# The third matrix's products in a gated MLP: sums formed in place, two chains interleaved

## The chip, the cores and the metric

One core of one Trainium2 chip runs the whole program. The metric is the device time of one execution in microseconds. TensorE (PE) multiplies, VectorE (DVE), ScalarE (ACT) and GpSimd (POOL) work on what it leaves; SyncE (SP) issues most transfers, GpSimd those that add to their destination.

## The reference

```python
X = np.fft.rfft(x, axis=1)                       # x: 2 x 3008 x 256
x = np.fft.irfft(X * (filt_r + 1j * filt_i), n=3008, axis=1)   # -> 6016 x 256
h = x @ w_in;  x = (h / (1 + exp(-h))) @ w_out   # first MLP, d_ff 2048
g = x @ w_gate                                   # second MLP, d_ff 1536
return (g / (1 + exp(-g)) * (x @ w_val)) @ w_out2
```

All in float32. The change touches the second MLP alone, above all its last product with `w_out2`.

## The kernel before, in words

A float32 product is made of three passes of a shorter format: each operand is split into a high part (ScalarE, line 1082 for the third matrix's) and a low part (VectorE, line 1087), and high times high, high times low and low times high are summed in PSUM. Products of matrices are cut in two both ways and made of seven products of half size instead of eight, with sums of operands ahead of them and sums of results behind them. The seven are numbered 1 to 7; `PARTS` names the three passes.

The second MLP, called the gated stage below, works in six blocks of tokens (five of 1024, the last of 896), each in six units `u` (`Pair`). A unit makes seven gate products and seven value products, 42 matmuls on line 827, each over half of the block's tokens. Their PSUM banks come in turn from `next_bank`. `Gate.p15` makes products 1 and 5, `p6`, `p3`, `p7` and `p4` the others; line 861 copies the first product into bank `y`, lines 888 and 894 add on VectorE, line 894 into a tile `c`. Value's product 4 of a unit (`tail`) and the multiplication behind it (`join`) stand in the next unit. What a unit leaves are two tiles, `a` (named `ga`, multiplied by value on lines 1030 and 1033) and `v.c` (lines 984 and 991), each holding two blocks of the operand of the third matrix.

Two units make a chain `c`: its seven products with `w_out2`, three passes and two halves of the contraction each, are 42 matmuls on line 1131, made while later units run. Each unit calls `tick` seven times; a tick queues three of these matmuls, and issues the splits, sums and weight loads that lie some ticks ahead of them. `product` takes matmuls from the queue between its own, one to two. A chain has 14 ticks. Before the change the operands 6 and 7 have a tile of their own, `x6`, filled by copies on SP's queue (lines 1067 and 1068, `copy7`); sums of operands are accumulating transfers on GpSimd's queue (line 1071, `more`). `after7` adds the products up, in part on GpSimd (line 1125).

The order on every engine is the order of the program. `side(k)` in a unit issues what `todo2` lists for step k: the loads of weight sums `wst` for a later unit (`load_s2`), loads and splits of the next block's input (`load_x2`, `prep_x2` on GpSimd, `split_x2`, whose low part is line 796), and `store2`, which transposes a finished half of an output block on VectorE (line 1169) and stores it with eight transfers of 128-byte pieces (line 1172). Tiles come from pools: `mp` with 33 buffers for most of the above, `late` with 9 for `ga` and the third matrix's weights `w7`. A new tile takes a buffer whose last user stands earlier in the program and waits for that user.

Of the kernel before, what the change touches and what calls it, by code (L numbers as in the profile page):

```python
# [119 lines left out]
def fft_filter_mlp_kernel(  # L120
# [61 lines left out]
    def mid(shape, name, dtype=F32):  # L182
        return mp.tile(shape, dtype, tag="mid", name=name)
# [349 lines left out]
            nc.sync.dma_start(d, w.bitcast(F32))  # L533
        ready.append([])

    AT7 = (1, 5, 6, 2, 7, 3, 4)
    MINUS = (5, 2, 4)

    def pieces(q, keys, v):
        w = mid([P, len(keys), 2, 2, P], "wst", F32R)  # L540
# [218 lines left out]
    def size2(t):  # L759
        return min(STEP2, NTOK - STEP2 * t)  # L760
# [77 lines left out]
    def bank(i):  # L838
        if i not in held:
            held[i] = psum("bk")  # L840
        return held[i]

    def next_bank(name):
        n = next(turns)
        return bank(4 + n % 4 if n < 6 else (4, 5, 6, 7, 3)[(n - 4) % 5])

    class Gate:

# [4 lines left out]
        def add(self, o, k, **kw):  # L853
            product(o, lambda part: self.w(k, part), self.x(k), **kw)
# [110 lines left out]
    class Pair:  # L965
# [15 lines left out]

        def upper(self):
            o = slice(self.g.n, 2 * self.g.n)
            nc.vector.tensor_tensor(self.v.c[:, o], self.v.c[:, o], self.g.c[:, o], op=ALU.mult)

        def tail(self):
            self.v.p4()

        def join(self):
            o = slice(0, self.g.n)  # L990
            nc.vector.scalar_tensor_tensor(
                self.v.c[:, o], self.v.y, -1.0, self.g.c[:, o], op0=ALU.mult, op1=ALU.mult
            )

        def run(self, old, side):
            g, v = self.g, self.v
            n, m = g.n, 2 * g.n

            owed[0], owed[1] = 0.0, max(0.5, (len(queue) + 24 * isinstance(old, Wide) + 1e-6) / 42)
            g.p15()  # L1000
            if old:
                old.tail()
            side(-1)
            tick()
            g.p6()
            if old:
                old.join()
            side(0)
            tick()
            g.add(g.a, 2, last=True)  # L1010
            a = late["p"].tile([P, STEP2], F32, tag="mid", name="ga")
            nc.scalar.activation(a[:, :n], g.a, AF.Silu)
            if isinstance(old, Wide):
                old.second()
            g.p3()
            nc.scalar.activation(a[:, n:m], g.b, AF.Silu)
            tick()
            g.p7()
            side(1)
            tick()  # L1020
            v.p15()
            nc.scalar.activation(g.c[:, n:], g.c[:, n:], AF.Silu)
            g.p4()
            nc.scalar.activation(g.c[:, :n], g.y, AF.Silu)
            side(2)
            tick()
            v.p6()
            side(3)
            v.add(v.a, 2, last=True)
            nc.vector.tensor_tensor(a[:, :n], v.a, a[:, :n], op=ALU.mult)  # L1030
            tick()
            v.p3()
            nc.vector.scalar_tensor_tensor(a[:, n:m], v.b, -1.0, a[:, n:m], op0=ALU.mult, op1=ALU.mult)
            v.p7()
            self.upper()
            raw[self.u] = a, v.c
            tick()
            side(4)
# [2 lines left out]
            self.tail()  # L1041
            self.join()

    raw, x6, ops7, w7, low7, done7 = {}, {}, {}, {}, {}, {}
    AHEAD = 4
    clock = [-21]
    def where(i):
        c, r = divmod(i, 14)
        return c, AT7[r // 2], r % 2

    def view(c, k, p):
        u = 2 * c + p
        n = size2(u // 6) // 2
        a, b = raw[u]
        if k in (6, 7):
            return x6[c, k][:, p, :n]
        v, l = {1: (a, 0), 5: (a, 1), 2: (b, 0), 4: (b, 0), 3: (b, 1)}[k]
        return v[:, n * l:n * l + n]

    def copy7(c, p):  # L1060

        if p == 0:
            for k in (6, 7):
                x6[c, k] = mid([P, 2, 512], "x6")
        u = 2 * c + p
        n = size2(u // 6) // 2
        nc.sync.dma_start(view(c, 7, p), raw[u][0][:, n:2 * n])
        nc.sync.dma_start(view(c, 6, p), view(c, 3, p))

    def more(c, k, j, p):  # L1070
        nc.gpsimd.dma_start(view(c, k, p), view(c, j, p), accum_op=ALU.add)  # L1071

    SUMS = {
        -9: [(copy7, 0)], -7: [(copy7, 1), (more, 5, 1, 0)], -6: [(more, 5, 1, 1)],
        -5: [(more, 7, 3, 0)], -4: [(more, 6, 5, 0)], -3: [(more, 6, 5, 1)], -2: [(more, 7, 3, 1)],
        5: [(more, 4, 6, 0)], 6: [(more, 4, 6, 1)],
    }

    def high7(c, k, p):
        x = ops7[c, k, p] = mid([P, 2, 512], "ho", F32R)  # L1080
# [3 lines left out]
    def lower7(c, k, p):  # L1084
        x, v = ops7[c, k, p], view(c, k, p)
        n = v.shape[-1]
        nc.vector.tensor_tensor(x[:, 1, :n], v, x[:, 0, :n], op=ALU.subtract)  # L1087
        if k == 4:
            del raw[2 * c + p]

    def load7(c, r):
        q = c % 3
        w = late["p"].tile([P, 2, 512], F32R, tag="mid", name="w7")
        n = min(2, 7 - 2 * r)
        nc.sync.dma_start(w[:, :n].bitcast(F32), d7[q][:, 2 * r:2 * r + n])
        for i in range(n):
            w7[c, AT7[2 * r + i]] = w[:, i].rearrange("p (j l c) -> p j l c", j=2, l=2)

    def after7(c, k):
        t, q = divmod(c, 3)  # L1100
        n = size2(t) // 2
        a, b, y = (bank(i)[:, :n] for i in range(3))
        add = lambda o, v, w: nc.vector.tensor_tensor(o, v, w, op=ALU.add)
        if k == 1:
            nc.scalar.copy(y, a)
        elif k == 5:
            done7[c] = sp.tile([P, 2, STEP2 // 2], F32, name="s")
            nc.scalar.copy(done7[c][:, 0, :n], b)
        elif k == 6:
            nc.scalar.copy(done7[c][:, 1, :n], y)  # L1110
        else:
            m, l, v = {2: (0, 0, a), 3: (0, 1, b), 7: (1, 1, y), 4: (1, 0, y)}[k]
            if (t, m) not in turned:
                turned[t, m] = mid([P, 2, 512], "oa")
            o = turned[t, m][:, l, :n]
            if k in (2, 4):
                if q == 0:
                    nc.scalar.copy(o, v)
                else:
                    add(o, v, o)  # L1120
            else:
                s = done7[c][:, int(k == 3), :n]
                add(o if q == 0 else s, v, s)
                if q:
                    nc.gpsimd.tensor_tensor(o, o, s, op=ALU.add)

    def product7(c, k, p, i):
        n = size2(c // 3) // 2
        o = bank({1: 0, 2: 0, 5: 1, 3: 1, 6: 2, 7: 2, 4: 2}[k])[:, :n]
        wpart, xpart = PARTS[i]  # L1130
        nc.tensor.matmul(  # L1131
            o, w7[c, k][:, p, wpart], ops7[c, k, p][:, xpart, :n],
            start=(k in (1, 5) and p == 0 and i == 0), stop=(k in (2, 3, 4) and p == 1 and i == 2),
            skip_group_check=True,
        )
        if p == 1 and i == 2:
            after7(c, k)

    CHAINS = 3 * NBLK2

    def tick():
        i = clock[0]
        clock[0] += 1
        inside = lambda i: 0 <= i < 14 * CHAINS
        if inside(i):
            queue.extend((product7, *where(i), k) for k in range(3))
        if inside(i + AHEAD - 1):
            lower7(*where(i + AHEAD - 1))
        if inside(i + AHEAD):
            high7(*where(i + AHEAD))  # L1150
        for o in (0, 14):
            c, r = divmod(i + o, 14)
            if 0 <= c < CHAINS and r - o in SUMS:
                for fn, *args in SUMS[r - o]:
                    fn(c, *args)
        if inside(i + 8):
            c, r = divmod(i + 8, 14)
            if r % 4 == 0:
                load7(c, r // 4)

    turned = {}

# [106 lines left out]
        at(END1 - 9 + k, prep_x2, 0, k)  # L1269
    for n, k in ((-7, 1), (-6, 2), (-5, 5), (-4, 6), (-2, 3)):  # L1270
        at(END1 + n, split_x2, 0, k, True)
    for n in range(4):
        at(END1 - 6 + n, load_s2, n // 2, KV[n % 2])

    todo2 = {}
    later = lambda u, k, fn, *args: todo2.setdefault((u, k), []).append((fn, args))
# [1 line left out]
        for n, args in enumerate((("g", q), ("v", q), ("a22", q))):  # L1278
            later(2 * q - 2, n, load_2, *args)
    for u in range(6 * NBLK2):  # L1280
        later(u, 1, load_s2, u + 2, "g")
        later(u, 4, load_s2, u + 2, "v")
    later(0, -1, split_x2, 0, 7)
    later(0, 0, split_x2, 0, 4)
    for t in range(1, NBLK2):
        for m in range(2):
            later(6 * t + 3 + m, 1, store2, t - 1, m)
        u = 6 * t - 6
        later(u + 2, 0, load_x2, t)
        later(u + 3, 1, prep_x2, t, 0)  # L1290
        later(u + 3, 3, prep_x2, t, 1)
        for k, n in ((0, 1), (1, 5), (3, 6)):
            later(u + 4, k, split_x2, t, n)

        for k, n in ((3, 2), (4, 3), (4, 7)):
            later(u + 5, k, split_x2, t, n)
        later(u + 6, 0, split_x2, t, 4)
# [33 lines left out]
    with tc.manual_schedule():  # L1331
# [191 lines left out]
            now.run(old, side)  # L1523
            old = now
        old.finish()
        while clock[0] < 14 * CHAINS:
            tick()
            drain(0)
        for m in range(2):
# [42 lines left out]
```

## Time and profile before

| what | value |
|---|---|
| median of 3 runs | 1214.3 us (1210.79 to 1216.09) |
| the profiled execution's own time | 1222.56 us |
| its span, first to last instruction | 1220.7 us |
| TensorE busy | 1139.6 us (93%) |
| VectorE, ScalarE, GpSimd busy | 832.6, 790.2, 453.1 us |
| DMA traffic | 237.93 MB, mean 195 GB/s |
| mean granted clock of TensorE | 0.971 of full |

A busy share is the time in which an engine had an instruction running, over the span. Matmuls overlap, so that TensorE's share says little about how fast they follow each other; the granted clock, the waits and the time of a unit say more. Durations below come from this one execution.

### The profile page before, as it was taken

How to read it: one execution, taken by the hardware profiler on the slowest of the kernel's cores; microseconds unless marked ns; L12 is line 12 of the kernel's file. 1: busy time of each engine (PE TensorE's matmuls, PEld its weight loads, DVE VectorE, ACT ScalarE, POOL GpSimd, SP SyncE). 2: the span in 40 equal slices, each digit the busy share in tenths (PEclk: the TensorE clock that was granted, in tenths of full speed). 3: DMA queues.
4: the chain of work that ended last, by engine and by line, in shares of the span. 5: the costliest groups of instructions: out<-in, count | busy, mean ns of one | idle time of the engine just before them, and what ended most of it. 6: DMA issues, size and time to landing. Idle time of an engine off the chain costs nothing.

```text
span 1220.7 us, 15570 instructions
## 1 busy us (share of the span) xinstructions
PE 1139.6 (93%) x4993; PEld 925.8 (76%) x4993; DVE 832.6 (68%) x1271; ACT 790.2 (65%) x1491; POOL 453.1 (37%) x423
## 2 busy tenths in 40 slices
PE   9999999999999999999989997888899699889984
PEld 7588888988888878888767776666677477668873
DVE  5977455665776867866557775776578567668755
ACT  5798666676776776765566575655676466566652
POOL 3558646543513625321041334134234223313323
PEclk9999999999999999999999998999999889899987
DMA  9964442463454554455398997898799879789886
GB/s 252 283 196 125 144 156 78 138 211 130 172 165 147 189 174 157 154 180 184 119 284 216 257 253 184 224 247 216 178 270 234 189 229 267 191 209 268 200 207 120
DMA packets 161217, 237.93 MB, mean 195 GB/s; under 512 B 60272, under 2 KB 92400, under 8 KB 161136
## 3 DMA queue, kind: packets, MB, share of 16 engines
q1 hardware_dynamic: 139952, 199.78, 51.2%
q0 software_dynamic: 20736, 36.97, 17.5%
q8 instruction: 39, 0.64, 0.2%
q14 instruction: 42, 0.34, 0.1%
q10 hardware_dynamic: 448, 0.20, 0.1%
HBM read 138.99 MB, written 42.47 MB: 149 GB/s over the span
## 4 chain that ended last, share of the span: by engine, by line
PE 67%; DMA 10%; DVE 9%; ACT 5%; issue 5%; POOL 2%; POOLq 0%; DVEq 0%; ACTq 0%
PE bk L827 15%; PE acc L740 14%; PE bk L1131 7%; PE acc L717 6%; PE h L667 6%; PE y L827 5%; DMA x<-ga 5%; PE xb L827 4%; PE xa L827 4%; DMA c<-x 3%; DMA ga<-ga 3%; PE s L209 2%; DVE ho L1087 2%; PE s L397 2%; PE s L206 1%
## 5 line engine op out<-in xcount | busy, mean ns | idle before, releaser
L827 PE MATMUL bk<-xo,wst 128*128 128x512 f32 (+1 forms) x864 | 288.4, 397 | 16.7 <-ACT bk L861 11.9
L1131 PE MATMUL bk<-ho,w 128*128 128x512 f32 (+1 forms) x756 | 286.3, 401 | 3.7 <-DVE ho L1087 2.3
L740 PE MATMUL acc<-h,w 128*128 128x512 f32 x768 | 283.6, 389 | 0.0
L827 PE MATMUL bk<-xo,w 128*128 128x512 f32 (+1 forms) x648 | 220.3, 407 | 46.0 <-DVE c L894 45.6
L827 PEld LDWEIGHTS bk<-xo,wst 128*128 128x128 f32 x864 | 166.3, 194 | 59.0 <-ACT bk L861 17.9
L827 PEld LDWEIGHTS bk<-xo,w 128*128 128x128 f32 x648 | 124.5, 196 | 84.6 <-DVE c L894 58.9
L1131 PEld LDWEIGHTS bk<-ho,w 128*128 128x128 f32 x756 | 148.6, 197 | 33.3 <-DVE ho L1087 3.3
L740 PEld LDWEIGHTS acc<-h,w 128*128 128x128 f32 x768 | 144.2, 188 | 29.6
L1071 POOL DMA_DIRECT2D ga<-ga x36 | 34.9, 969 | 227.6 <-DMA x<-ga 83.4
L717 PE MATMUL acc<-h,w 128*128 128x512 f32 (+1 forms) x384 | 95.4, 376 | 0.0
L1071 POOL DMA_DIRECT2D c<-x x36 | 31.4, 957 | 153.5 <-DVE ho L1087 152.9
L1082 ACT CAST ho<-c 128x512 fp32r<-128x512 f32 (+1 forms) x108 | 64.5, 610 | 36.7 <-DVE ho L1087 18.5
L667 PE MATMUL h<-xh,w 128*128 128x512 f32 (+1 forms) x248 | 83.6, 379 | 0.3 <-POOL w L503 0.3
L717 PEld LDWEIGHTS acc<-h,w 128*128 128x128 f32 x384 | 71.2, 188 | 11.2
L1087 DVE TENSOR_TENSOR ho<-c,ho 128x512 fp32r<-128x512 f32 (+1 forms) x108 | 74.4, 700 | 7.2 <-ACT ho L1082 7.1
L1082 ACT CAST ho<-x 128x512 fp32r<-128x512 f32 (+1 forms) x72 | 44.5, 619 | 49.2 <-DMA x<-ga 34.0
L827 PE MATMUL xb<-xo,wst 128*128 128x512 f32 x192 | 74.7, 391 | 1.0 <-DVE h L921 1.0
L827 PE MATMUL xa<-xo,w 128*128 128x512 f32 x192 | 75.3, 394 | 0.0
L827 PE MATMUL y<-xo,wst 128*128 128x512 f32 x192 | 74.7, 389 | 0.0
L675 DVE TENSOR_TENSOR h<-h,h 128x512 fp32r<-128x512 f32 (+1 forms) x64 | 41.4, 655 | 47.9 <-ACT h L674 46.5
L1087 DVE TENSOR_TENSOR ho<-x,ho 128x512 fp32r<-128x512 f32 (+1 forms) x72 | 51.9, 723 | 18.4 <-ACT ho L1082 18.3
L888 DVE TENSOR_TENSOR bk<-bk,u 128x512 f32<-128x512 f32 (+1 forms) x72 | 49.2, 684 | 21.4 <-PE bk L827 19.7
(157 smaller groups left out, 2341.7 us busy)
## 6 DMA issues: line engine op xcount, KB each, us to landing
w<-d SPq DMA_DIRECT2D x54, 512.0 KB, 6.4
wst<-ds_g SPq DMA_DIRECT2D x36, 512.0 KB, 5.4
wst<-ds_v SPq DMA_DIRECT2D x36, 512.0 KB, 6.2
wst<-ds SPq DMA_DIRECT2D x32, 512.0 KB, 4.6
x<-ga SPq DMA_DIRECT2D x30, 256.0 KB, 4.6
x<-c SPq DMA_DIRECT2D x30, 256.0 KB, 4.6
ga<-ga POOLq DMA_DIRECT2D x30, 256.0 KB, 6.4
x<-c POOLq DMA_DIRECT2D x30, 256.0 KB, 7.8
```

What stands on the lines that cost most here:

```text
L209: nc.tensor.matmul(o, csp[:k, mp_, r:r + n], x[xp_], start=(i == 0), stop=(i == 2))
L397: nc.tensor.matmul(ps[:, col:col + n], zt_of[c // 2, g][:, 3 * (c % 2) + t, :], c4[:, o:o + n], start=(t == 0), stop=(t == 2), skip_group_ ...
L667: nc.tensor.matmul(ps[:, :n], wt[key, f // 4, g][:, wpart, o:o + P], x[xpart][:, g, :n], start=(g == 0 and k == 0), stop=(g == 1 and k == 2),)
L675: nc.vector.tensor_tensor(h[:, 1, :n], u[:, :n], h[:, 0, :n], op=ALU.subtract)
L717: nc.tensor.matmul(a[:, :n], w[:, wpart, o:o + 128], h[:, xpart, :n], start=(f == 0 and k == 0), stop=(f == 15 and k == 2),)
L740: nc.tensor.matmul(a, w[:, wpart, o:o + 128], h[xpart][:, n * l:n * l + n], start=(f == 0 and k == 0), stop=(end and k == 1), skip_group_c ...
L827: nc.tensor.matmul(o, w(wpart), x[:, xpart, :o.shape[-1]], start=(first and k == 0), stop=(last and k == 2), skip_group_check=True,)
L888: nc.vector.tensor_tensor(self.b, self.b, self.u2, op=ALU.add)
L1071: nc.gpsimd.dma_start(view(c, k, p), view(c, j, p), accum_op=ALU.add)
L1082: nc.scalar.copy(x[:, 0, :v.shape[-1]], v)
L1087: nc.vector.tensor_tensor(x[:, 1, :n], v, x[:, 0, :n], op=ALU.subtract)
L1131: nc.tensor.matmul(o, w7[c, k][:, p, wpart], ops7[c, k, p][:, xpart, :n], start=(k in (1, 5) and p == 0 and i == 0), stop=(k in (2, 3, 4) ...
```

## The change

Operands 5, 6, 4 and 7 are formed in the buffers of `ga` and `v.c` themselves, by four sums for each half (1 += 7, then 1 += 3, then 7 += 3, then 4 += 6); the copies and `x6` are gone. The products run in another order, with 3, 7 and 4 one period of 14 ticks later than the others, between products of the next chain, and each operand is split its own number of ticks ahead (`EARLY`). The signs of some weights and of two products of gate and value are turned to fit. The third matrix has four PSUM banks of its own, gate and value share the other four. Results are added up by VectorE and ScalarE alone. The last chain's sums are VectorE's. Loads of `wst` are issued one unit ahead instead of two, at steps 0 and 3, and `store2` stands at other steps. After the last unit 33 ticks follow instead of 21.

```diff
-    AT7 = (1, 5, 6, 2, 7, 3, 4)
-    MINUS = (5, 2, 4)
+    AT7 = (1, 5, 2, 6, 3, 7, 4)
+    MINUS = (1, 6, 7, 3)
...
     def next_bank(name):
-        n = next(turns)
-        return bank(4 + n % 4 if n < 6 else (4, 5, 6, 7, 3)[(n - 4) % 5])
+        return bank(4 + next(turns) % 4)
...
-            nc.vector.tensor_tensor(self.v.c[:, o], self.v.c[:, o], self.g.c[:, o], op=ALU.mult)
+            nc.vector.scalar_tensor_tensor(
+                self.v.c[:, o], self.v.c[:, o], -1.0, self.g.c[:, o], op0=ALU.mult, op1=ALU.mult
+            )
...
-    AHEAD = 4
-    clock = [-21]
+    ORDER7 = (3, 1, 7, 5, 2, 6, 4)
+    BACK7 = (3, 7, 4)
+    EARLY = {3: 4, 1: 8, 7: 6, 5: 6, 2: 4, 6: 4, 4: 10}
+    clock = [-19]
...
     def view(c, k, p):
...
-        if k in (6, 7):
-            return x6[c, k][:, p, :n]
-        v, l = {1: (a, 0), 5: (a, 1), 2: (b, 0), 4: (b, 0), 3: (b, 1)}[k]
-        return v[:, n * l:n * l + n]
-
-    def copy7(c, p):
-
-        if p == 0:
-            for k in (6, 7):
-                x6[c, k] = mid([P, 2, 512], "x6")
-        u = 2 * c + p
-        n = size2(u // 6) // 2
-        nc.sync.dma_start(view(c, 7, p), raw[u][0][:, n:2 * n])
-        nc.sync.dma_start(view(c, 6, p), view(c, 3, p))
+        v, l = {1: (0, 0), 5: (0, 0), 6: (0, 0), 7: (0, 1), 2: (1, 0), 4: (1, 0), 3: (1, 1)}[k]
+        return raw[u][v][:, n * l:n * l + n]
 
     def more(c, k, j, p):
-        nc.gpsimd.dma_start(view(c, k, p), view(c, j, p), accum_op=ALU.add)
-
-    SUMS = {
-        -9: [(copy7, 0)], -7: [(copy7, 1), (more, 5, 1, 0)], -6: [(more, 5, 1, 1)],
-        -5: [(more, 7, 3, 0)], -4: [(more, 6, 5, 0)], -3: [(more, 6, 5, 1)], -2: [(more, 7, 3, 1)],
-        5: [(more, 4, 6, 0)], 6: [(more, 4, 6, 1)],
-    }
+        o, v = view(c, k, p), view(c, j, p)
+        if c < CHAINS - 1:
+            nc.gpsimd.dma_start(o, v, accum_op=ALU.add)
+        else:
+            nc.vector.tensor_tensor(o, o, v, op=ALU.add)
+
+    SUMS = ((-5, 1, 7), (1, 1, 3), (4, 7, 3), (8, 4, 6))
...
+    def bank7(c, k):
+        n = size2(c // 3) // 2
+        return bank({1: 0, 2: 0, 5: 2, 3: 2}.get(k, 1 + 2 * (c % 2)))[:, :n]
...
         if k == 1:
-            nc.scalar.copy(y, a)
-        elif k == 5:
+            nc.scalar.copy(bank7(c, 6), v)
+            return
...
+        if k == 5:
             done7[c] = sp.tile([P, 2, STEP2 // 2], F32, name="s")
-            nc.scalar.copy(done7[c][:, 0, :n], b)
-        elif k == 6:
-            nc.scalar.copy(done7[c][:, 1, :n], y)
+        if k in (5, 6):
+            s = done7[c][:, int(k == 6), :n]
+            if q == 0:
+                nc.scalar.copy(s, v)
+            else:
+                add(s, v, o)
+        elif k in (3, 7):
+            add(o, v, done7[c][:, int(k == 3), :n])
+        elif q == 0:
+            nc.scalar.copy(o, v)
         else:
...
-            if k in (2, 4):
-                if q == 0:
-                    nc.scalar.copy(o, v)
-                else:
-                    add(o, v, o)
-            else:
-                s = done7[c][:, int(k == 3), :n]
-                add(o if q == 0 else s, v, s)
-                if q:
-                    nc.gpsimd.tensor_tensor(o, o, s, op=ALU.add)
+            add(o, v, o)
...
-    for n in range(4):
-        at(END1 - 6 + n, load_s2, n // 2, KV[n % 2])
+    for n in range(2):
+        at(END1 - 6 + n, load_s2, 0, KV[n])
...
-        later(u, 1, load_s2, u + 2, "g")
-        later(u, 4, load_s2, u + 2, "v")
+        later(u, 0, load_s2, u + 1, "g")
+        later(u, 3, load_s2, u + 1, "v")
...
-            later(6 * t + 3 + m, 1, store2, t - 1, m)
+            later(6 * t + 3 + 2 * m, 2 - m, store2, t - 1, m)
...
-        while clock[0] < 14 * CHAINS:
+        while clock[0] < 14 * CHAINS + 14:
             tick()
             drain(0)
```

`tick` and `where` follow `ORDER7`, `BACK7` and `EARLY`; loads of `w7` are issued at ticks -6, 2, 8 and 18 of a chain instead of every fourth.

## Rows read from the trace of the kernel before

**Rows 1.** The page: busy us, share of the span and instructions.

```profile
PE 1139.6 (93%) x4993; PEld 925.8 (76%) x4993; DVE 832.6 (68%) x1271; ACT 790.2 (65%) x1491; POOL 453.1 (37%) x423
```

**Rows 2.** Stretches: length, busy PE, PEld, DVE, ACT, POOL (instructions), clock, DMA share, GB/s.

```profile
626.04:646.15 20.11, 16.86 (x61) 12.76 (x60) 10.42 (x15) 10.56 (x20) 9.74 (x9) 0.83 1.07 329
625.81:1188.11 562.30, 501.84 (x2082) 401.34 (x2081) 391.72 (x607) 348.26 (x663) 172.25 (x173) 0.95 0.88 227
917.40:931.80 14.40, 14.40 (x65) 11.80 (x64) 10.61 (x18) 10.32 (x19) 4.84 (x5) 1.00 1.02 275
1124.40:1137.78 13.38, 13.38 (x64) 11.83 (x63) 9.89 (x17) 9.61 (x19) 5.41 (x6) 1.00 1.03 281
739.53:781.90 42.37, 33.12 (x127) 25.80 (x126) 23.27 (x38) 23.25 (x43) 7.96 (x10) 0.88 0.82 201
1165.30:1187.02 21.72, 16.98 (x64) 13.95 (x63) 10.61 (x20) 10.80 (x24) 6.68 (x8) 0.84 0.91 206
691.90:709.80 17.90, 15.63 (x64) 11.34 (x63) 12.70 (x19) 9.89 (x19) 5.68 (x6) 1.00 0.91 217
763.07:781.91 18.84, 15.95 (x64) 12.78 (x63) 12.08 (x20) 12.31 (x23) 1.72 (x2) 0.91 0.76 191
1188.11:1220.70 32.59, 17.16 (x65) 13.11 (x64) 19.92 (x32) 8.82 (x18) 11.11 (x11) 0.75 0.62 126
```

**Rows 3.** TensorE's waits from 600 us on: us in total, times, longest.

```profile
PE bk L827 <- DVE c L894: 45.6, 28, 5.9
PE bk L827 <- ACT bk L861: 11.9, 11, 2.0
```

**Rows 4.** Timeline in the first slow pair: start, duration, instruction, [idle before <- releaser].

```profile
737.51 1.30 POOL L776 TENSOR_TENSOR xr<-x,xr 128x512 f32<-128x512 f32 x1
738.75 1.76 POOL L1071 DMA_DIRECT2D c<-x  x2
...
745.64 0.69 DVE L894 TENSOR_TENSOR c<-bk,s 128x512 f32<-128x512 f32 x1 [4.95 <-DMA c<-x]
...
768.16 1.65 PE L827 MATMUL bk<-xo,w 128*128 128x512 f32 x3 [2.89 <-DVE c L894]
```

**Rows 5.** Waits of ScalarE and VectorE for sums, from 600 us on.

```profile
ACT ho L1082 <- DMA x<-ga: 34.0, 20, 3.9
...
ACT ho L1082 <- DMA ga<-ga: 21.9, 9, 6.2
DVE c L894 <- DMA c<-x: 21.6, 4, 6.2
```

**Rows 6.** Timeline around two sets of eight stores, SP and POOL.

```profile
733.96 4.14 SPq L1172 DMA_DIRECT2D out_dram<-ob  x8
...
756.00 10.47 SPq L1172 DMA_DIRECT2D out_dram<-ob  x8
...
757.50 1.21 POOL L1071 DMA_DIRECT2D x<-c  x1
```

**Rows 7.** The page's transfers: issues, KB each, median us from issue to landing.

```profile
wst<-ds_g SPq DMA_DIRECT2D x36, 512.0 KB, 5.4
wst<-ds_v SPq DMA_DIRECT2D x36, 512.0 KB, 6.2
...
ga<-ga POOLq DMA_DIRECT2D x30, 256.0 KB, 6.4
x<-c POOLq DMA_DIRECT2D x30, 256.0 KB, 7.8
```

**Rows 8.** Timeline of one addition on GpSimd and VectorE's instructions around it.

```profile
694.51 0.68 DVE L1087 TENSOR_TENSOR ho<-ga,ho 128x512 fp32r<-128x512 f32 x1
...
695.74 2.38 DVE L1087 TENSOR_TENSOR ho<-ga,ho 128x512 fp32r<-128x512 f32 x1
695.96 1.59 POOL L1125 TENSOR_TENSOR oa<-oa,s 128x512 f32<-128x512 f32 x1
```

**Rows 9.** Timeline of the tail: the last transposes.

```profile
1209.55 2.22 DVE L1169 STREAM_TRANSPOSE ob<-oa 128x448 f32<-128x448 f32 x4
```

More of the change, by code (lines that the diff above doesn't have):

```diff
@@ L990, in join @@
             o = slice(0, self.g.n)
-            nc.vector.scalar_tensor_tensor(
-                self.v.c[:, o], self.v.y, -1.0, self.g.c[:, o], op0=ALU.mult, op1=ALU.mult
-            )
+            nc.vector.tensor_tensor(self.v.c[:, o], self.v.y, self.g.c[:, o], op=ALU.mult)
         def run(self, old, side):
@@ L1029, in run @@
             v.add(v.a, 2, last=True)
-            nc.vector.tensor_tensor(a[:, :n], v.a, a[:, :n], op=ALU.mult)
+            nc.vector.scalar_tensor_tensor(a[:, :n], v.a, -1.0, a[:, :n], op0=ALU.mult, op1=ALU.mult)
             tick()
             v.p3()
-            nc.vector.scalar_tensor_tensor(a[:, n:m], v.b, -1.0, a[:, n:m], op0=ALU.mult, op1=ALU.mult)
+            nc.vector.tensor_tensor(a[:, n:m], v.b, a[:, n:m], op=ALU.mult)
             v.p7()
@@ L1042, in finish, with where @@
             self.join()
-    raw, x6, ops7, w7, low7, done7 = {}, {}, {}, {}, {}, {}
-    AHEAD = 4
-    clock = [-21]
-    def where(i):
-        c, r = divmod(i, 14)
-        return c, AT7[r // 2], r % 2
+    raw, ops7, w7, done7 = {}, {}, {}, {}
+    CHAINS = 3 * NBLK2
+    ORDER7 = (3, 1, 7, 5, 2, 6, 4)
+    BACK7 = (3, 7, 4)
+    EARLY = {3: 4, 1: 8, 7: 6, 5: 6, 2: 4, 6: 4, 4: 10}
+    clock = [-19]
+    def where(i, k=None):
+        c, r = divmod(i, 14)
+        if k is None:
+            k = ORDER7[r // 2]
+        elif ORDER7[r // 2] != k:
+            return None
+        c -= k in BACK7
+        return (c, k, r % 2) if 0 <= c < CHAINS else None
     def view(c, k, p):
@@ L1087, in lower7 @@
         nc.vector.tensor_tensor(x[:, 1, :n], v, x[:, 0, :n], op=ALU.subtract)
-        if k == 4:
+        if k == 7:
+            raw[2 * c + p] = None, raw[2 * c + p][1]
+        elif k == 4:
             del raw[2 * c + p]
     def load7(c, r):
-        q = c % 3
         w = late["p"].tile([P, 2, 512], F32R, tag="mid", name="w7")
         n = min(2, 7 - 2 * r)
-        nc.sync.dma_start(w[:, :n].bitcast(F32), d7[q][:, 2 * r:2 * r + n])
+        nc.sync.dma_start(w[:, :n].bitcast(F32), d7[c % 3][:, 2 * r:2 * r + n])
         for i in range(n):
             w7[c, AT7[2 * r + i]] = w[:, i].rearrange("p (j l c) -> p j l c", j=2, l=2)
+    def bank7(c, k):
+        n = size2(c // 3) // 2
+        return bank({1: 0, 2: 0, 5: 2, 3: 2}.get(k, 1 + 2 * (c % 2)))[:, :n]
     def after7(c, k):
@@ L1101, in after7 @@
         n = size2(t) // 2
-        a, b, y = (bank(i)[:, :n] for i in range(3))
+        v = bank7(c, k)
         add = lambda o, v, w: nc.vector.tensor_tensor(o, v, w, op=ALU.add)
         if k == 1:
-            nc.scalar.copy(y, a)
-        elif k == 5:
-            done7[c] = sp.tile([P, 2, STEP2 // 2], F32, name="s")
-            nc.scalar.copy(done7[c][:, 0, :n], b)
-        elif k == 6:
-            nc.scalar.copy(done7[c][:, 1, :n], y)
-        else:
[L1112 to L1115, printed above, removed]
-            if k in (2, 4):
-                if q == 0:
-                    nc.scalar.copy(o, v)
-                else:
-                    add(o, v, o)
-            else:
-                s = done7[c][:, int(k == 3), :n]
-                add(o if q == 0 else s, v, s)
-                if q:
-                    nc.gpsimd.tensor_tensor(o, o, s, op=ALU.add)
+            nc.scalar.copy(bank7(c, 6), v)
+            return
+        m, l = {2: (0, 0), 3: (0, 1), 6: (0, 1), 7: (1, 1), 5: (1, 1), 4: (1, 0)}[k]
+        if (t, m) not in turned and k in (2, 3, 7, 4):
+            turned[t, m] = mid([P, 2, 512], "oa")
+        o = turned[t, m][:, l, :n] if (t, m) in turned else None
+        if k == 5:
+            done7[c] = sp.tile([P, 2, STEP2 // 2], F32, name="s")
+        if k in (5, 6):
[8 more added lines that the diff above has]
+            nc.scalar.copy(o, v)
+        else:
+            add(o, v, o)
     def product7(c, k, p, i):
         n = size2(c // 3) // 2
-        o = bank({1: 0, 2: 0, 5: 1, 3: 1, 6: 2, 7: 2, 4: 2}[k])[:, :n]
+        o = bank7(c, k)
         wpart, xpart = PARTS[i]
@@ L1137, in product7 @@
             after7(c, k)
-    CHAINS = 3 * NBLK2
     def tick():
@@ L1143, in tick @@
         clock[0] += 1
[L1144 to L1159, printed above, removed]
+        at7 = where(i)
+        if at7:
+            queue.extend((product7, *at7, k) for k in range(3))
+        for k in ORDER7:
+            at7 = where(i + EARLY[k] - 1, k)
+            if at7:
+                lower7(*at7)
+        for k in ORDER7:
+            at7 = where(i + EARLY[k], k)
+            if at7:
+                high7(*at7)
+        for o, k, j in SUMS:
+            c, r = divmod(i - o, 14)
+            if r < 2 and 0 <= c < CHAINS:
+                more(c, k, j, r)
+        for r, o in enumerate((-6, 2, 8, 18)):
+            c, x = divmod(i - o, 14)
+            if x == 0 and 0 <= c < CHAINS:
+                load7(c, r)
     turned = {}
```

1 line of the change is left out of this document (removed).

## The prediction

> **What bounds the kernel now.** I read the busy shares first: TensorE is busy 93% of the span [rows 1], so work moved off other engines pays only where TensorE stands still. The table by stretches says where that is [rows 2]. The change touches only the gated stage, from about 586 us to the end, in which each of 36 units runs 42 gate and value matmuls and, from the fourth unit on, 21 matmuls of the third matrix. A clean unit takes 14.4 us at a clock of 1.00, a clean unit of the last, narrower block 13.4 us. The 33 units from 625.8 to 1188.1 us would take 27 x 14.4 + 6 x 13.4 = 469 us if all were clean; they take 562.3. So about 93 us are lost there, and the tail behind them takes 32.6 us. TensorE reads 501.8 us busy of the 562.3, but that counts pipelined matmuls of some 0.39 us each; the unit times are the better measure.
>
> Where are the 93 us? In each of four blocks, the two units around the second store of the previous block are slow together: 42.4 us where two clean ones take 28.8 (the row is the first of four alike) [rows 2]. With some 13.8 us each that is 55; unit 35 loses 8 more (21.7 against 13.4). The fourth unit loses 5.7 and one later 3.5 (20.1 and 17.9 against 14.4). The other 22 lose about 21 us together.
>
> What releases TensorE there is nearly always VectorE's line 894, the sum after product 7: 45.6 us in 28 waits, the longest 5.9; ScalarE's copy on line 861 adds 11.9 [rows 3]. VectorE is not slow by itself, it is held up in order. In the timeline, L894 wants to write a new tile `c` and stands 4.95 us until an accumulating transfer into `c` from `x` lands, and TensorE starts again after it [rows 4]. The buffer is one that `x6` has just given up, and that transfer was issued late, behind GpSimd's `prep_x2` subtractions. Elsewhere ScalarE's split waits for sums: 34.0 us for those into `x`, 21.9 us for those into `ga`, and VectorE 21.6 us for those into `c` [rows 5]. Both copies stand on SP's queue, and there eight stores of `store2` took 10.47 us with sums in flight, but 4.14 us when none had been issued [rows 6].
>
> **The change, part by part.**
>
> *Copies and `x6` go.* Two per unit, 72 in all, each with an issue on SP and a landing to wait for. The chain copy, sum, sum becomes sum, sum. The time for one sum is that of the row, 6.4 us to landing [rows 7] after 0.9 us of issue [rows 4]. The room it gets: the first sum (1 += 7) stands 5 ticks ahead of the split of operand 5, the second (1 += 3) 5 ticks ahead of that of 6, the other two 8 ticks. A unit has 7 ticks, so 5 ticks are 10.3 us. VectorE's lower half must be done first, about 1 us behind the tick: 1 + 0.9 + 6.4 = 8.3 us, inside 10.3. With the 7.8 us of the slower sums [rows 7] it is 9.7, still inside. In the old order the sum into 6 had 4 ticks (8.2 us) and the one into 4 had 3 (6.2 us). So ScalarE's 56 us of waits for sums mostly end, and the wait of L894 for `x6`'s buffer has no cause left. I take the store units' 55 + 8 us off, less 1.1 us in each of five for the block's operand splits (VectorE's L796 behind ScalarE), which stay: **-58**, bounds -40 (half of ScalarE's lateness has another cause) to -63.
>
> *GpSimd's 24 additions go, VectorE gets 24 more.* Each GpSimd addition took 1.6 us, and where one ran, VectorE's L1087, otherwise 0.68, took 2.38 us [rows 8]. That is in the unit of 17.9 us. Its 3.5 us and some 9 us more in seven units where the same meeting of the two shows are to be had; two additions in each of 12 chains cost VectorE 24 x 0.6 = 14 us, mostly in its idle third (391.7 busy of 562.3 [rows 2]), but some just ahead of L894. Net **-7**, bounds -13 to +7. ScalarE loses 24 copies of 0.58 us, off the path: nothing.
>
> *Signs* move from some operations to others of the same form count: nothing.
>
> *Weights come one unit ahead, not two, and the stores move.* Now SP matters. Value's `wst` for the next unit is issued at step 3, after 30 of 42 gate matmuls, 10.2 us into a unit, and its first user is product 5 of value in the next unit, at 14.4 + 8.2 = 22.6 us. Landing takes 6.2 us [rows 7]; without stores it has 6 us to spare. The gate's own has about the same. But `store2` now goes just ahead of it. Store 0 of a block stands at step 2 of unit 6t+3: transposes and queue start it at about 11.8 us. With 4.1 us of stores the load is issued at 15.9 and lands at 22.1: no wait. With 10.5 us it lands at 28.5: a wait of 5.9 us. Store 1 stands at step 1 of unit 6t+5, starts at 8.7 us (VectorE's lag and the first transpose put 1.6 us between step and store, as ahead of the store at 733.96 [rows 6]), and the same two prices give landings of 19.0 and 25.4 us: 0 to 2.8 us. In the new order the sums into 7 and 4 are in flight around both. I take 7 us for eight stores, between the two rows: 2.5 us of wait behind store 0, none behind store 1. Five blocks have store 0: 12.5 us, with cooling 20. A wait also cools the clock (the pair of 42.4 us has 0.88 granted, a mix of 1.2 and 2.4 GHz); its second unit, of 18.8 us, waits 2.9 us at L894 and loses 4.4 in all [rows 2, 4], so I add 1.5 each. Behind the waiting product stand all of value's products and the third matrix's, and VectorE and ScalarE run dry; behind the late load on SP stand two `w7` loads, which have 8 ticks to spare: **+21**, bounds 0 and 5 x 5.9 + 4 x 2.8 + 9 x 1.5 = +54.
>
> *Four rotating PSUM banks instead of five.* Two reuses get close: gate's bank `b` follows value's `a` of the unit before (L1030), gate's `y` follows value's `b` (L1033). L1033 stands just ahead of L894 on VectorE, and product 6, which needs ScalarE's copy into `y`, comes three matmuls after the tail that needs L894; so the copy hides behind the wait that is there already. Product 5 has 13 matmuls, 3 us, after value's product 2. I take 0.15 us a unit, **+5**, bounds 0 and +0.6 us (one VectorE operation late) x 33 = +20.
>
> *The products' order.* Each PSUM bank of the third matrix now has four slots or more between read and next use, before two. TensorE waits little on L1131 in the steady part, so: nothing.
>
> *The tail.* The chains end 33 ticks after the last unit instead of 21, with 25 of them carrying products, and chain 17's eight sums are VectorE's. Counting what VectorE still has to do there: 20 lower halves, 8 sums, 12 additions, 2 joins, 42 operations at 0.55 us (four transposes take 2.22 [rows 9]) = 23.1 us, and 1.8 us for the last two products and their addition: 24.9 us. Now it is 1188.1 to 1209.6, 21.5 us. **+3**, bounds 0 (ScalarE waited for sums there too, which ends) to +8.
>
> Sum: -58 - 7 + 21 + 5 + 3 = -36; and the fourth unit, whose first sums came late behind weight loads, gives back perhaps 4 of its 5.7: **-40**. The profiled execution took 1222.6 us around its span of 1220.7 and becomes 1182; its time lies 8.3 us above the median of the three runs, so the median goes from 1214.3 to **1174**.
>
> A rule speaks against the change here. The stores were slow with sums in flight and quick without [rows 6]. The Trainium skill, "DMA: Bandwidth & Descriptors", section "Queues, rings and completion order", says that each DMA engine takes turns between the queue rows that have work, packet by packet; the two kinds of row agree with it. By that rule the stores are slow at both new places, since sums run beside them at both, the rival of slow stores below, 1207; by the row without sums the term would be nought.
>
> **Rivals.**
> - *Forecast*, 1174 within 12: the store units heal, store 0 costs a short wait. Chance 0.40.
> - *No wait for weights at all*: eight stores stay near 4.1 us, the term of 21 goes: 1153. For it, SP no longer carries the copies; against it, sums beside the stores. 0.22.
> - *Slow stores at both places*: 10.5 us each, +54 instead of +21: 1207 if all else holds; 1200 if the loads land in the 5.4 us of the gate's [rows 7] (5 x 5.1 + 4 x 2.0 + 13.5 = 47). 0.18.
> - *The change does not cure the stall*: tiles still take buffers just given up, and VectorE or ScalarE waits on a different one (a stored `ob`, a matmul's `ho`). Half of the 58 stays: 1203. 0.10.
> - *Slower*: value's weights late in every unit. Their room is 12.4 us from step 3; a landing above that makes TensorE wait once a unit. At 14.3 us it is 1.9 us x 33 = 61 us on top of the sum without store waits (1153): slower than now from there on. Against it: the median is 6.2. For it: SP issues in order and each load must wait for a buffer. 0.10.
>
> **Numbers.** 1174. The first three and half of the fourth fill the range: from 1146 (bounds of the second) to 1206. Faster by over 0.5% (6 us, about what a measurement of this kernel tells from no change: its three runs spread over 5.3 us): below 1208, 0.84; within, 0.07; slower, 0.09.
>
> **What would show it.** No SP rows of copies; ScalarE's waits for sums below 15 us; no VectorE wait for a landing ahead of L894; pairs of store units near 32 us instead of 42; TensorE or its weight loads waiting for `wst` behind store 0. L1087 without spans above 2 us. Wrong would be: units without stores above 16 us (banks, VectorE), `wst` as the releaser in every unit, or a tail above 38 us.

## The result, and the profile after

The changed kernel takes 1168.5 us in the median of three runs (1166.25 to 1172.48), 0.963 of the time before (95% interval 0.958 to 0.969): 46 us less. The prediction was 1174, range 1146 to 1206, faster with a chance of 0.84. The profiled execution took 1168.46 us around a span of 1165.7.

On the page, busy time and share of each engine after:

```profile
PE 1118.7 (96%) x4993; PEld 914.3 (78%) x4993; DVE 839.8 (72%) x1306; ACT 777.8 (67%) x1467; POOL 410.0 (35%) x388
```

TensorE issues the same 4993 matmuls; its share rises from 93% [rows 1]. The stretches that answer to [rows 2]: all units from the fourth to the last gate matmul, a clean unit, the four store pairs, the fourth unit, the unit that had held a GpSimd addition, unit 35, the fifth block's second store unit, the tail (columns as there):

```profile
626.02:1130.91 504.89, 480.65 (x2070) 388.94 (x2069) 394.45 (x626) 337.48 (x641) 142.96 (x154) 0.99 0.85 212
873.00:887.53 14.53, 14.31 (x63) 11.52 (x62) 10.47 (x18) 10.15 (x19) 4.36 (x5) 1.00 0.93 232
732.33:765.67 33.34, 29.95 (x128) 23.27 (x126) 24.80 (x41) 23.45 (x45) 6.98 (x8) 1.00 0.84 198
824.02:857.37 33.35, 29.94 (x128) 23.26 (x126) 24.81 (x41) 23.45 (x45) 6.98 (x8) 1.00 0.85 199
916.26:949.60 33.34, 29.95 (x128) 23.27 (x126) 24.79 (x41) 23.45 (x45) 6.98 (x8) 1.00 0.84 199
1008.25:1043.87 35.62, 32.65 (x128) 25.32 (x126) 24.41 (x41) 23.58 (x45) 6.98 (x8) 0.90 0.86 197
626.02:643.61 17.59, 14.71 (x55) 11.05 (x54) 9.31 (x14) 10.08 (x19) 9.44 (x9) 0.90 0.77 188
689.33:703.61 14.28, 14.28 (x65) 11.82 (x63) 10.74 (x18) 10.30 (x19) 4.36 (x5) 1.00 0.90 220
1111.45:1129.84 18.39, 14.93 (x65) 12.81 (x63) 13.27 (x25) 11.60 (x24) 5.23 (x6) 0.91 0.82 160
1023.68:1043.87 20.19, 17.70 (x65) 13.73 (x63) 14.97 (x25) 12.70 (x24) 4.36 (x5) 0.83 0.76 169
1130.91:1165.67 34.76, 18.51 (x78) 14.94 (x76) 24.08 (x45) 8.06 (x16) 0.00 (x0) 0.79 0.37 99
```

The gain lies in the units: 562.3 us became 504.9. The four store pairs took 42.4, 42.1, 45.0 and 42.8 us before and 33.3, 33.4, 33.3 and 35.6 after, 37 us less in all; unit 35 gave 3.3, the unit of 17.9 us 3.6, the fourth 2.5, and the other 11 us are spread thin. The tail grew from 32.6 to 34.8 us.

Waits from 600 us on, of TensorE, ScalarE and VectorE (us in total, times, longest):

```profile
PE bk L827 <- DVE c L893: 10.0, 14, 1.5
PE bk L827 <- ACT bk L860: 8.0, 9, 2.4
PE bk L827 <- DVE ga L1029: 5.9, 4, 1.5
...
ACT ho L1077 <- DMA ga<-ga: 20.2, 12, 4.3
...
DVE xo L796 <- ACT xo L793: 32.1, 19, 4.5
```

L893 is what was L894, L860 was L861, L1077 was L1082. TensorE's wait for the sum after product 7 fell from 45.6 to 10.0 us and that for ScalarE's copy from 11.9 to 8.0 [rows 3], VectorE's 21.6 us of waits for landings ahead of it are gone, and ScalarE's waits for sums fell from 55.9 to 20.2 us [rows 5]. TensorE waits nowhere for `wst`. What is left of a store pair is seen in the timeline of units 9 to 11 (queue SP, VectorE and TensorE, [idle before <- releaser]):

```profile
729.78 4.81 SPq L1172 DMA_DIRECT2D out_dram<-ob  x8
734.70 0.46 SPq L646 DMA_DIRECT2D wst<-ds_v  x1
...
748.82 0.69 DVE L796 TENSOR_TENSOR xo<-xr,xo 128x512 fp32r<-128x512 f32 x1 [4.48 <-ACT xo L793]
...
750.03 0.68 DVE L1029 SCALAR_TENSOR_TENSOR ga<-bk,ga 128x512 f32<-128x512 f32 x1
...
750.76 0.50 PE L827 MATMUL bk<-xo,wst 128*128 128x512 f32 x1 [1.51 <-DVE ga L1029]
...
760.09 7.84 SPq L1172 DMA_DIRECT2D out_dram<-ob  x8
```

VectorE stands 4.5 us at the low part of a block operand (L796), which it reached before ScalarE had made the high part (L793); L1029 behind it frees a bank late, and TensorE loses 1.5 us. Of the page's transfers one row (issues, KB, median us to landing, which was 6.2 before [rows 7]):

```profile
wst<-ds_v SPq DMA_DIRECT2D x36, 512.0 KB, 4.8
```

### The profile page after: what moved, and what is told of

Its sections match the earlier page's. It is cut to its first block, busy times and chain, and to the rows that moved or that the text cites. A ratio compares the mean times of both kernels' runs of the same rounds, so it can differ in the third digit from the quotient of the medians.

```text
span 1165.7 us, 15384 instructions
## 1 busy us (share of the span) xinstructions
PE 1118.7 (96%) x4993; PEld 914.3 (78%) x4993; DVE 839.8 (72%) x1306; ACT 777.8 (67%) x1467; POOL 410.0 (35%) x388
## 4 chain that ended last, share of the span: by engine, by line
PE 79%; DVE 7%; ACT 5%; DMA 4%; issue 4%; POOL 1%; DVEq 0%; ACTq 0%; SPq 0%; POOLq 0%
PE bk L827 21%; PE acc L740 15%; PE bk L1130 10%; PE acc L717 7%; PE h L667 6%; PE y L827 6%; PE xb L827 4%; PE xa L827 4%; DMA ga<-ga 3%; PE s L209 2%; PE s L206 2%; DVE ho L1082 2%; PE s L397 2%; PE s L282 1%; ACT ho L1077 1%
## 5 line engine op out<-in xcount | busy, mean ns | idle before, releaser
L827 PE MATMUL bk<-xo,wst 128*128 128x512 f32 (+1 forms) x864 | 280.4, 390 | 15.5 <-ACT bk L860 8.0
L1130 PE MATMUL bk<-ho,w 128*128 128x512 f32 (+1 forms) x756 | 278.1, 393 | 4.5 <-DVE ho L1082 2.3
L827 PE MATMUL bk<-xo,w 128*128 128x512 f32 (+1 forms) x648 | 213.3, 396 | 10.5 <-DVE c L893 10.0
L1130 PEld LDWEIGHTS bk<-ho,w 128*128 128x128 f32 x756 | 144.4, 192 | 31.4 <-DVE ho L1082 3.6
L1068 POOL DMA_DIRECT2D ga<-c x68 | 59.4, 1064 | 181.6 <-DVE ho L1082 181.4
L1077 ACT CAST ho<-ga 128x512 fp32r<-128x512 f32 (+1 forms) x144 | 87.0, 614 | 35.0 <-DMA ga<-ga 20.2
L1068 POOL DMA_DIRECT2D ga<-ga x34 | 30.2, 892 | 198.8 <-DVE c L992 57.3
L1082 DVE TENSOR_TENSOR ho<-ga,ho 128x512 fp32r<-128x512 f32 (+1 forms) x144 | 95.7, 672 | 2.3 <-ACT ho L1077 2.3
L1082 DVE TENSOR_TENSOR ho<-c,ho 128x512 fp32r<-128x512 f32 (+1 forms) x108 | 80.7, 749 | 2.6 <-ACT ho L1077 2.6
L1077 ACT CAST ho<-c 128x512 fp32r<-128x512 f32 (+1 forms) x108 | 63.9, 611 | 13.2 <-PE bk L1130 9.0
L860 ACT COPY bk<-bk 128x512 f32<-128x512 f32 (+1 forms) x72 | 41.2, 572 | 40.9 <-DVE ga L1032 24.7
```

Of the source, the lines that this page charges most:

```text
L827: nc.tensor.matmul(o, w(wpart), x[:, xpart, :o.shape[-1]], start=(first and k == 0), stop=(last and k == 2), skip_group_check=True,)
L860: nc.scalar.copy(self.y, self.a)
L1068: nc.gpsimd.dma_start(o, v, accum_op=ALU.add)
L1077: nc.scalar.copy(x[:, 0, :v.shape[-1]], v)
L1130: nc.tensor.matmul(o, w7[c, k][:, p, wpart], ops7[c, k, p][:, xpart, :n], start=(k in (1, 5) and p == 0 and i == 0), stop=(k in (2, 3, 4) ...
```

## The experiments

Two theories stood after the result. *Copies*: the store units healed because the copies no longer stand behind the stores on SP and `x6` is gone. *Buffers*: operands, results, weights `wst` and `x6` all come from one pool of 33 buffers; with two units' weights loaded ahead the pool is used up, and a new `c` (L894) has to wait for whatever is released last. Loading one unit ahead leaves two more buffers free. The kernel before was timed again beside each group of runs (medians 1216.6 to 1217.4 us); ratios are to it, with the 95% interval.

**One part alone in the kernel before: the shorter lead.**

```diff
-    for n in range(4):
-        at(END1 - 6 + n, load_s2, n // 2, KV[n % 2])
+    for n in range(2):
+        at(END1 - 6 + n, load_s2, 0, KV[n])
...
-        later(u, 1, load_s2, u + 2, "g")
-        later(u, 4, load_s2, u + 2, "v")
+        later(u, 0, load_s2, u + 1, "g")
+        later(u, 3, load_s2, u + 1, "v")
```

> The kernel before with the weight sums loaded one unit ahead at steps 0 and 3, as in the changed kernel; nothing else. Theory of the copies (the prediction's): the slow pairs come from copies that stand behind the stores on SP and from sums that land late, so they stay above 40 us and the time between 1206 and 1220. Theory of the buffers: around the stores the pool of 33 is used up, and whatever asks for a tile waits for whoever gives one back; two weight tiles fewer alive heal most of it: pairs below 36 us, no VectorE wait for a landing at L894, the time below 1192.

1179.4 us, 0.970 (0.967 to 0.973): 37 of the 46 us, with every copy, `x6` and the stores where they were. The first store pair, and the waits from 600 us on:

```profile
738.84:772.74 33.90, 30.09 (x127) 23.26 (x126) 22.42 (x37) 22.56 (x43) 7.13 (x9) 1.00 1.04 269
```

```profile
PE bk L827 <- DVE c L894: 14.7, 23, 1.1
...
ACT ho L1082 <- DMA x<-ga: 24.4, 16, 3.8
...
ACT ho L1082 <- DMA ga<-ga: 19.1, 8, 6.7
```

The pair takes 33.9 us instead of 42.4, and no wait of VectorE for a landing is left ahead of L894, though ScalarE still waits 43.5 us for sums (55.9 before). So those waits were not what held the store units, and the copies theory falls as the main cause. The short lead also has the price that the prediction named, but not behind the first stores: TensorE waits 5.0 us for `wst` in the fourth unit and 2.5 in the last.

```profile
PE bk L827 <- DMA wst<-ds_v: 7.5, 2, 5.0
```

**The same with two buffers fewer.** If the gain came from when the loads are issued, the size of the pool would not matter.

```diff
-    mp = pool("mp", 33)
+    mp = pool("mp", 31)
```

> The kernel before with weight sums one unit ahead, and the pool cut from 33 to 31 buffers, so that just the two saved tiles are taken away again. Theory of the buffers: L894's waits for a landing come back, the two units around the second store take 40 us or more together, the time is 1205 or above. Rival, the loads' new time is what helps (they no longer meet copies and sums on the DMA engines): it stays within 6 us of the 1179 of 33 buffers.

1259.1 us, 1.037 (1.034 to 1.040), 80 us more than with 33. The first store pair, and the waits:

```profile
747.95:794.67 46.72, 34.39 (x128) 26.25 (x127) 23.09 (x38) 23.42 (x44) 9.88 (x11) 0.85 0.73 183
```

```profile
PE bk L827 <- ACT bk L861: 37.6, 14, 6.8
PE bk L827 <- DVE c L894: 36.4, 25, 3.1
...
ACT ho L1082 <- DMA c<-x: 30.7, 6, 7.5
...
DVE c L894 <- DMA c<-x: 11.1, 4, 2.9
```

The slow pair is back, and worse. With the loads issued at the same steps, two buffers are worth 80 us: buffers, not the time of the loads, carry the gain. VectorE's waits ahead of L894 are back too, but most of the stall sits at ScalarE now, four times 6.8 to 7.5 us. The first of the four (POOL and ScalarE):

```profile
749.09 1.76 POOL L1071 DMA_DIRECT2D c<-x  x2
...
756.43 0.62 ACT L1082 CAST ho<-c 128x512 fp32r<-128x512 f32 x1 [7.41 <-DMA c<-x]
```

By its place in the program this split makes the high part of operand 3, into which no sum goes. Its operand lies in the tile that the first of the two transfers writes, which landed at 753.5; the split went on only when the second had landed as well, at 756.4. What the two have in common is `x6`, which both read. So ScalarE stood for a buffer, that of `x6`, at its new tile `ho`, as VectorE does at its new `c` in the kernel before. Why 31 buffers with the short lead come out 43 us above the kernel before, which holds two more weight tiles in two more buffers, is shown no further than this: two engines stand there instead of one.

**The stores moved, alone.**

```diff
-            later(6 * t + 3 + m, 1, store2, t - 1, m)
+            later(6 * t + 3 + 2 * m, 2 - m, store2, t - 1, m)
```

> The kernel before with the stores of an output block at the changed kernel's steps (half 0 at step 2 of unit 6t+3, half 1 at step 1 of unit 6t+5); nothing else. Theory of the place: the old place beside the next block's operand sums and splits makes the slow pairs, so they shrink below 36 us and the time goes below 1192. Theories of the copies and of the buffers: the copies still stand behind the stores and no buffer is saved, so 1204 to 1220, with the loss in one or two units later at most.

1236.6 us, 1.017 (1.012 to 1.021): slower. The first pair:

```profile
736.70:781.23 44.53, 34.34 (x127) 26.22 (x126) 22.84 (x37) 23.01 (x43) 7.86 (x9) 0.89 0.75 181
```

```profile
DVE c L894 <- DMA c<-x: 20.1, 4, 5.2
```

The pair is no quicker with the stores moved (42.4 before), and the waits of VectorE for a landing ahead of L894 stay: the place of the stores does not heal it.

**The additions on VectorE, alone; four banks, alone; the additions with the shorter lead.**

```diff
-                    nc.gpsimd.tensor_tensor(o, o, s, op=ALU.add)
+                    add(o, o, s)
```

> The kernel before with the 24 additions of line 1125 on VectorE instead of GpSimd; nothing else. The prediction's term: VectorE's long L1087 (2.38 us) ends, the unit of 17.9 us falls below 15.5, and the time falls by 7 (bounds: 13 less to 7 more), to some 1207. Rival: the additions on VectorE stand ahead of L894 and cost as much as they give: 1212 to 1221.

> The kernel before with weight sums one unit ahead and line 1125's additions on VectorE: two of the change's parts, with copies, x6 and five banks left. If these two are nearly all of the change: 1168 to 1176. If sums in place give something of their own (ScalarE's waits for sums, some 44 us in the kernel with the loads alone, become 20): 1176 to 1182, and 8 us or more are left to them.

```diff
-        return bank(4 + n % 4 if n < 6 else (4, 5, 6, 7, 3)[(n - 4) % 5])
+        return bank(4 + n % 4)
```

> The kernel before with four PSUM banks in turn for gate and value instead of five; nothing else. The prediction's term: 5 us more (bounds 0 and 20), some 1219, with waits of TensorE for L1030 or of ScalarE's L861 for L1033. Rival: the fifth bank was never what anything waited for: within 3 us of before and no new releaser.

The additions alone: 1218.05 us, 1.0005 (0.998 to 1.003). With the shorter lead: 1180.4 against 1179.4 without. They are worth nothing either way that these runs can show. The unit of 17.9 us still takes 18.1 with no addition on GpSimd in it; TensorE waits 2.5 us for L894 there:

```profile
690.88:708.95 18.07, 15.37 (x65) 11.43 (x63) 11.85 (x20) 9.90 (x19) 4.39 (x5) 1.00 0.90 216
```

Four banks: 1214.2 us, 0.997 (0.995 to 0.999), a little quicker. TensorE's waits from 600 us on:

```profile
PE bk L827 <- DVE c L894: 32.3, 25, 4.9
PE bk L827 <- ACT bk L861: 11.1, 11, 1.6
PE bk L827 <- DVE ga L1030: 5.8, 4, 1.5
```

The new wait for L1030 is the one that the changed kernel shows too; a second new one, 3.7 us for L1012, it does not show. Both are outweighed by L894's, which shrinks from 45.6 to 32.3, so the path pays nothing.

**All parts but the sums in place and the new order.** The shorter lead, the additions, the moved stores and the four banks together, in the kernel before (their diffs are above).

> The kernel before with all parts of the change but the sums in place and the products' order: weight sums one unit ahead, stores at the new steps, line 1125's additions on VectorE, four banks. If the loads' new time (two buffers) is the whole of the gain: 1165 to 1173. If copies, x6 and the old order still cost what the changed kernel saves beyond it: 1176 to 1186, with ScalarE's waits for sums above 30 us.

1196.0 us, 0.981 (0.977 to 0.986): outside both expectations, 16 us above the shorter lead with the additions (1180.4) and 28 above the whole change (22 by the ratios). Against the kernel with the shorter lead and the additions, units 13, 19, 25 and 31, two behind each second store, take 73 us instead of 60, and the tail 39.9 instead of 34.9. Here are the copies that the prediction had in mind. Queue SP and POOL of this kernel around unit 12 (the view cuts off the first of the eight stores):

```profile
767.95 4.53 SPq L1172 DMA_DIRECT2D out_dram<-ob  x7
...
774.45 0.47 SPq L1067 DMA_DIRECT2D x<-ga  x1
...
776.33 0.95 SPq L1067 DMA_DIRECT2D x<-ga  x1
...
780.07 0.86 POOL L1071 DMA_DIRECT2D ga<-ga  x1 [9.33 <-DMA x<-ga]
```

and of the one with the stores at their old place:

```profile
769.19 0.47 SPq L1067 DMA_DIRECT2D x<-ga  x1
...
773.20 0.86 POOL L1071 DMA_DIRECT2D ga<-ga  x1 [3.22 <-DMA x<-ga]
```

At the new place the copies stand behind the stores; 5.3 us later goes the first copy and 6.9 us later the first sum, and ScalarE's waits for sums into `ga` grow from 15.7 to 35.0 us. So the copies behind stores do cost time where the stores have been moved. In the changed kernel, which has no copies, the same four units take 57 us; that the new place is harmless there is read from this, not tried with the stores at their old steps. The sums in place with the new order are worth 22 to 28 us on top of these parts; the whole change is 8 to 12 us quicker than the shorter lead with or without the additions, a difference hardly larger than the interval of the changed kernel's three runs.

**Every store of blocks 0 to 4 issued twice,** in the changed kernel; the second goes to a spare buffer in DRAM. It tells whether weights behind a long row of stores are late by the prediction's working.

```diff
+                if t < NBLK2 - 1:
+                    nc.sync.dma_start(spare[...], o[...])
                 nc.sync.dma_start(
```

> The changed kernel with each store of blocks 0 to 4 issued twice, once into a spare buffer in DRAM, so that SP issues 16 transfers of 128-byte pieces ahead of value's weights instead of 8. The prediction's price of a late load: stores of 9.6 to 15 us put the load some 5 us past its room behind half 0 and some 7 behind half 1, 5 x 5 + 4 x 7 and some cooling: 1168 + 50 to 65 = 1218 to 1233, with TensorE released by wst. Rival: SP's lateness is covered by the other work: below 1180.

1223.7 us, 1.006 (1.004 to 1.009), 55 above the changed kernel. The waits, and the timeline behind the first row of 16, which begins at 729.35 (lines are one or two lower down here):

```profile
PE bk L828 <- DMA wst<-ds_v: 46.2, 9, 6.8
```

```profile
738.11 1.30 SPq L1178 DMA_DIRECT2D out_dram<-ob  x1
739.52 1.33 SPq L647 DMA_DIRECT2D wst<-ds_v  x1
...
747.51 1.19 PE L828 MATMUL bk<-xo,wst 128*128 128x512 f32 x2 [6.75 <-DMA wst<-ds_v]
```

The row takes 10.1 us, near the prediction's slow price of 10.5, and TensorE then waits 6.75 us where the working said 5.9. The mechanism holds; the price of eight stores was too high.

**The last chain's sums as transfers,** in the changed kernel.

```diff
-        if c < CHAINS - 1:
+        if c < CHAINS:
```

> The changed kernel with the last chain's eight sums as transfers like all others. The prediction's tail counts VectorE's operations; if VectorE bounds the tail, eight sums fewer would save 4 us: 1164. If the chain sum, split, sum bounds it, each landing of 4.5 us or more stands in a row twice where VectorE's sum took 0.6: the tail goes from 35 to 40 us or more, 1173 to 1180.

1172.2 us, 0.962 (0.957 to 0.967). From the end of unit 35 the tail takes 37.8 us instead of 35.8, but the ratio doesn't differ from 0.963. Inconclusive; at most a small gain lies in VectorE's sums there.

**The block operand's low part one step later.** L796 stood 32 us behind ScalarE; here it is issued a step behind the high part.

```diff
-            later(u + 4, k, split_x2, t, n)
+            later(u + 4, k, split_x2, t, n, True)
...
+                due, lag[:] = lag[:], []
...
+                for fn in due:
+                    fn()
```

> The changed kernel with the low part of the next block's splits (L796) issued one step after the high part, so that VectorE does not stand behind ScalarE there. In the changed kernel VectorE idles 34.5 us in 20 such waits, and units 6t+5 and 6t take 17.5 and 15.4 us. If these waits are what is left: those units fall to 15 and 14.4, and the time to 1150 to 1160. Rival: VectorE only waits elsewhere, or the additions pile up behind: within 5 us of 1168.

1166.3 us, 0.960 (0.956 to 0.963): within the noise of the changed kernel, as the rival said. The unit behind the pair takes 14.6 us instead of 15.4, but the pair's second unit, and a new wait in it, give that back:

```profile
744.97:765.72 20.75, 17.75 (x64) 13.74 (x63) 13.51 (x23) 12.84 (x24) 4.36 (x5) 0.84 0.76 167
```

```profile
ACT ho L1077 <- DVE xo L796: 3.9, 1, 3.9
```

ScalarE now waits at a new tile `ho` for the late L796, whose result is no operand of its split: it looks like a buffer that comes free late again, though only this wait shows it.

**A best version,** twice: the low parts deferred except operand 6's, the last block's first stores seven ticks earlier and its last ones on two queues in turn; then also with operand 6 split a step earlier.

```diff
-        for k, n in ((0, 1), (1, 5), (3, 6)):
-            later(u + 4, k, split_x2, t, n)
+        for k, n in ((0, 1), (1, 5), (3, 6)):
+            later(u + 4, k, split_x2, t, n, n != 6)
...
+            if clock[0] == 14 * CHAINS + 7:
+                store2(NBLK2 - 1, 0)
...
-                nc.sync.dma_start(
+                queues[i % 2].dma_start(
```

> The changed kernel with L796 one step after its high part, except for operand 6, whose input buffer a ScalarE split waited for when it was given back late; and the last block's half 0 stored as soon as product 3 of the last chain is added, half 1's eight stores issued from two queues in turn. Units 6t fall from 15.4 to 14.6 and 6t+5 stay at 17.5: 4 us; the end saves the half of 8 us of stores: 4 to 6 us. 1157 to 1162. Rival: deferred lows hold buffers longer and ScalarE waits for them again: 1164 to 1170.

> As the run before it, with operand 6 of the next block split one step earlier (step 2 of unit 6t+4, after GpSimd's subtractions are long done). If the wait of ScalarE's split of 6 for a buffer is what holds VectorE 4.5 us there, another place finds another buffer: units 6t+5 fall from 17.5 to 15.5, 1150 to 1156. Rival: it only meets another buffer's owner: within 4 us of the run before it.

1165.2 us each, 0.957 (0.953 to 0.960): both hopes missed, both rivals met. From the end of unit 35 the tail takes 32.6 us instead of 35.8. In the second version (first the pair's second unit, then the unit two later):

```profile
744.99:760.33 15.34, 14.60 (x65) 11.75 (x64) 13.62 (x23) 11.94 (x23) 4.36 (x5) 1.00 0.84 200
774.94:795.45 20.51, 17.09 (x64) 13.60 (x63) 10.93 (x18) 10.74 (x20) 4.36 (x5) 0.83 0.90 216
```

The first heals (15.3 instead of 17.5 us) and the other, 14.3 in the changed kernel, loses 6: ScalarE waits up to 4.5 us there for a sum into `ga`. Both versions have the lowest medians, 3 us under the changed kernel, which these intervals do not tell apart.

Not run: the kernel before with two buffers more and its weights two units ahead, the direct counterpart of the run with 31; the copies and `x6` taken out with the weights still two units ahead; and the changed kernel with the stores at their old steps. Read from the program alone, the changed kernel with weights two units ahead or with 32 buffers would ask for a buffer that only later work releases.

## Why the prediction was right, and where its reasons were not

**Direction and size: right**; 1168.5 lies in the forecast's own range (1174 within 12) and between it and its rival without waits (1153). Part of the closeness is luck, as the next paragraphs say: a cause that was not the main one, terms that came to nought and cancel in part, and a starting point on the high side.

**Copies and `x6`, -58: the total holds, the places and the cause do not.** The units without the fourth gave 55 us, but the units that the term named, the four pairs and unit 35, gave 40, its smaller bound; the other 15 came from units that it left alone. The step "the wait of L894 for `x6`'s buffer has no cause left" took the late transfer for the fault, and the copies' removal for the cure. The runs show that the tile waits because no buffer is free: the shorter lead alone gives 37 us and leaves the copies, and two buffers fewer take it back with 43 more. The row that should have warned is [rows 4]. L894 there is value's in unit 9, and it starts at 745.64, when the second of the two transfers has landed (745.5). That transfer has nothing to do with what L894 computes, and the unit's last tick issues it, behind L894 in the program. The description ahead says that a new tile takes a buffer whose last user stands earlier in the program; here it does not. A tile that waits for such a user had no free buffer to take, so the question was how many tiles are alive, not why one transfer is late. Taking out `x6` frees buffers as well; whether that would have healed the store units by itself, with weights two units ahead, no run shows. The term also foresaw ScalarE's waits below 15 us; they are 20.2.

**GpSimd's additions, -7: nought** (1.0005 alone). L1087's 2.38 us [rows 8] were seen, but the unit's end hung on other waits.

**Weights, +21: nought; mis-sized.** (Its own terms, 12.5 and five times 1.5, add up to 20.) Eight stores took 4.8 us at store 0, not 7, and a load lands in 4.8 (the median), not 6.2: it is issued at 734.70 and wanted at 732.3 + 8.2 = 740.5. Store 1 started 11.9 us into its unit, not 8.7, and took 7.8 us, and the load behind it was still in time. With twice the stores the predicted wait appears. The rival of slow stores at both places needed 10.5 us at each.

**Banks, +5: nought** (0.997 alone); the wait exists, 5.9 us in all, and takes the place of part of L893's. **Tail, +3:** +2.2. **The fourth unit, -4:** 2.5, and it now has 54 matmuls instead of 60.

**The starting point.** The sum was carried down from the profiled execution, 8.3 us above its median, and the 8.3 kept. The changed kernel's profiled execution lies on its median, so the span fell by 55.0 us and the median by 45.8. By spans the steps (-40) are 15 us short: weights and banks (+26) and the additions (-7) were nought, and without them the steps give -59. So the forecast came within 6 us of the median because 9 of the 15 us went into the starting point.

The rule weighed against the change is in the Trainium skill, "DMA: Bandwidth & Descriptors", section "Queues, rings and completion order": each DMA engine takes turns between the queue rows that have work. The trace agrees in part: the second set of stores, with five sums issued between 754.86 and 762.4, took 7.8 us; the first, with two between 727.4 and 731.9, took 4.8. Neither reached 10.5.

## What to carry to other kernels

When an engine stands at a new tile until some transfer lands, ask whether that transfer has to do with what the engine computes; if not, count the live tiles of the pool before blaming the transfer. A shorter prefetch lead can pay, as it frees buffers: here 37 us. A unit that is slow where the stores stand need not owe it to them: move them alone, and see. Parts of one change need not add: moving the stores costs 16 to 20 us while copies share their queue, and the changed kernel, which has no copies, shows no such loss.

## What the hardware showed that was not expected

A short stall has two prices. Unit 29 of the changed kernel stood 1.39 us at L1029 and took 20.2 us at a granted clock of 0.83 (a mix of the two levels); units 11, 17 and 23 stood 1.51 us at the same place, took 17.5 us and kept 1.00. TensorE's only other wait in each of the four units is 1.1 us for L893, so the 2.7 us between them go with the clock; the runs don't show what decided it.

GpSimd's addition more than tripled a VectorE operation beside it (0.68 to 2.38 us [rows 8]), and removing all 24 changed the time by no more than 0.3% (the ends of the interval).
